# The last weight loads of the first MoE are held back from place 18 of their order instead of place 15

## The chip, the cores and the metric

The kernel runs as one program on one core of a Trainium2 chip. The metric is the device time of the program in microseconds (us). The core has five engines that run side by side and meet through semaphores: PE (TensorE: matrix products into PSUM), DVE (VectorE: elementwise work), ACT (ScalarE: activations), POOL (GpSimd: elementwise work on SBUF) and SP, which here only issues DMA transfers. Each engine and each DMA queue works its instructions off in the order in which they stand in the program; whoever waits holds up all that stands behind it on the same engine.

## What is computed

Three stages follow each other, all in float32 with weights that arrive as 64-bit numbers:

```python
# 1. delta-rule attention, state S per head, t = 0..767
y[t] = q[t] @ S
S    = S + beta[t] * outer(k_n[t], v[t] - k_n[t] @ S)      # k_n: k by its norm
# 2. first MoE: x is the attention's output, 3072 tokens x 384
h = x @ w_in                                              # 384 -> 2048
g = where(h >= 1, h, where(h <= -1, 0, (h + 1)**2 / 4))
x = g @ w_out                                             # 2048 -> 384
# 3. second MoE
xn = x / sqrt(mean(x*x) + 1e-6) * rms_g
out = (silu(xn @ w_gate) * (xn @ w_val)) @ w_out          # 384 -> 1536 -> 384
```

## The kernel before

**Attention.** The 768 steps are cut into 12 chunks of 64, and each chunk into two units, one for each pair of batches, so there are 24 units; unit u belongs to chunk u // 2. Within a unit the recurrence becomes matrix products on PE plus the inverse of a triangular matrix. `a_gram` makes the products of the keys with each other (tile `gk`), scales them (`al`) and stores them to DRAM (`scr_a`). `inverse` works on groups of units (units 0 and 1, units 2 and 3, then four at a time): it loads the stored products as `nt`, runs 31 pairs of steps on POOL (L530, L536), and stores the result (`scr_x`, `scr_a`). `a_mz` reads it back as `tx` and `g` and scales it on POOL into `wt` (L557, L558); `a_mw` multiplies once more on PE (`mg`) and finishes `wt` on DVE (L585). `b_vn` scales the values on POOL (`kvb`, L612). `b_gs` multiplies queries and keys on PE (`gs`, L623) and masks the result on DVE (L629, L633); two such halves to a unit, four to a chunk. `b_tr`, `b_x`, `b_ds` and `b_xT` follow on PE (`tr`, `px`, `ds`, `xps`).

**First MoE.** The weights of one slice f of 128 hidden columns come as two tiles, i = 0 for `w_in` and i = 1 for `w_out`. `w_dec` loads one (`wst`, L265, 384 KB) and decodes it: two activations on ACT, three steps on DVE (L286, L287, L297), one activation, three products on PE (`wlo`, L315 to L317), and one copy (L320 on ACT or L322 on DVE). The number f + 3 i (SK is 3) is the tile's **place** in the order of decoding. From place 10 on, the loads land in four staging buffers that are used in turn, so a load must wait until the DVE step L297 of the tile four loads before it has read its buffer. `m1` then runs for 12 blocks of 256 tokens, one block to a chunk, and for 16 slices each: nine products into `hps`, the gate on ACT and DVE (L773, L781), nine products into `acc`. A group of nine is written "block.slice" below. There are two `hps` buffers, each free again when DVE has done L773. While blocks 0 to 11 run, the weights of the second MoE are decoded too (`w_dec` with n = 2: L286, L287, L290, L291 on DVE) and stored for later.

**Second MoE.** From about 660 us on PE has products alone (`gv`, `acc`), with all weights decoded.

**What sets the order.** All work of attention, first MoE and decoding is written as generators that yield stages. A planner (`Flow`) keeps an estimate of each engine's time and of free buffers, picks the stage that can start next, by its priority, and so fixes the order of instructions on every engine when the program is built. A stage may start when its `needs` are done; a need is therefore an entry in the planner's bookkeeping, no semaphore of its own on the chip. Because each choice depends on those before it, an entry that is changed at one place can move everything that is planned after it.

The loads of `w_dec` for the first MoE have such a need from some place on: `("a_gram", EARLY - 1)`, with EARLY = 8, which is done when the key products of unit 7 have been sent to DRAM. The line is 255. It is the only thing that the diff touches.

Of the kernel before, what the change touches and what calls it, by code (L numbers as in the profile page):

```python
# [160 lines left out]
def kernel_body(  # L161
# [89 lines left out]
    def w_dec(n, f, i):  # L251
        if n == 2:
            needs = [("w_dec", 1, NF1 - 1, 1)]
        else:
            needs = [("a_gram", EARLY - 1)] if f + SK * i > 14 else []
        if n == 1:
            needs = needs + ([("inv0", 1 if f + SK * i < 9 else 19)] if f + SK * i >= 4 else [])
        me = ("w_dec", n, f, i)
# [76 lines left out]
    EARLY = 8  # L335
# [516 lines left out]
    SK = 3  # L852
# [20 lines left out]
    with tc.manual_schedule():  # L873
# [28 lines left out]
        for f in range(NF1):  # L902
            for i in range(2):
                fl.add(f + SK * i + (-14), w_dec, 1, f, i)
        for n, x in enumerate(w2q):
            fl.add(16 + 4 * n, w_dec, 2, *x)
# [168 lines left out]
```

## Time and profile before

| | us |
|---|---|
| median of 3 runs | 1153.7 |
| lowest and highest run | 1152.92, 1155.39 |
| the profiled execution, its own time | 1154.3 |
| its span from first to last instruction | 1152.4 |
| PE busy | 1107.5 |
| DVE busy | 661.8 |
| ACT busy | 569.9 |
| POOL busy | 286.3 |

The profiled execution lies 0.6 us above the median, and 1.9 us of its time lie outside its span. PE is busy nearly all of the time, so what is to be looked for are the few microseconds in which it is not, and those in which it runs at half its clock.

### The profile page before, as it was taken

Reading aid. Unit: us, or ns where it says so; the run is one execution under the profiler, and the core shown is the slowest. Engines: PE = TensorE matmul, PEld = TensorE weight load, DVE = VectorE, ACT = ScalarE, POOL = GpSimd, SP = SyncE. Lnnn points to the kernel's source line nnn. Section 1 sums busy time; section 2 is a strip of 40 time slices with the busy share of each in tenths; the row PEclk is TensorE's granted clock in tenths of the full one; section 3 lists DMA queues with packets and bytes.
Section 4 is the critical chain, followed back from the end, with each engine's and each line's share of the span. In section 5 each row is a group of like instructions: output and inputs, shape, how many; then the busy total and the mean of one; then the engine's idle time right before and its main releaser. Section 6 shows DMA issues by size and latency. Waiting matters only on the chain.

```text
span 1152.4 us, 27191 instructions
## 1 busy us (share of the span) xinstructions
PE 1107.5 (96%) x11224; PEld 996.4 (86%) x11224; DVE 661.8 (57%) x1337; ACT 569.9 (49%) x1360; POOL 286.3 (25%) x479
## 2 busy tenths in 40 slices
PE   8979999999999999999999999999999999999998
PEld 7857888899998999899999999788888888888887
DVE  6797876786877876785775453443433333333333
ACT  4677877765765767567665464222212122122212
POOL 3282865858348114811000000000000000000000
PEclk9989999999999999999999999999999999999999
DMA  7945587784786556385440564001001010010000
GB/s 219 285 143 138 148 262 197 231 208 153 185 224 185 128 199 181 114 206 172 151 148 2 183 207 167 10 23 37 19 1 46 10 37 19 1 46 10 28 1 28
DMA packets 165099, 136.97 MB, mean 119 GB/s; under 512 B 115056, under 2 KB 126064, under 8 KB 164976
## 3 DMA queue, kind: packets, MB, share of 16 engines
q1 hardware_dynamic: 141536, 132.31, 38.2%
q10 hardware_dynamic: 23440, 2.93, 1.7%
q8 instruction: 88, 1.44, 0.5%
q14 instruction: 35, 0.29, 0.1%
HBM read 100.88 MB, written 34.34 MB: 117 GB/s over the span
## 4 chain that ended last, share of the span: by engine, by line
PE 74%; DVE 11%; ACT 4%; POOL 3%; DMA 3%; issue 2%; SPq 1%; DVEq 0%; POOLq 0%; ACTq 0%
PE acc L736 9%; PE gv L736 8%; PE gv L737 8%; PE gv L738 8%; PE acc L737 8%; PE acc L738 8%; PE hps L736 4%; PE hps L737 4%; PE hps L738 4%; PE gs L623 2%; POOL xi L536 2%; PE px L691 2%; POOL tmp L530 2%; PE tr L678 1%; DVE da L287 1%
## 5 line engine op out<-in xcount | busy, mean ns | idle before, releaser
L752 ACT ACTIVATE xh<-fix 128x512 fp32r<-128x512 f32 x72 | 45.5, 632 | 333.7 <-PE acc L738 328.4
L753 DVE TENSOR_TENSOR xl<-fix,xh 128x512 fp32r<-128x512 f32 x72 | 49.9, 694 | 270.6 <-ACT xh L752 270.6
L736 PE MATMUL hps<-xh,w 128*128 128x256 f32 x576 | 167.5, 291 | 9.9 <-DVE w__1065 L773 2.2
L737 PE MATMUL acc<-g,w 128*128 128x256 f32 x576 | 164.7, 286 | 10.6 <-DVE g L781 10.4
L736 PE MATMUL acc<-g,w 128*128 128x256 f32 x576 | 167.8, 291 | 2.7 <-ACT g L779 2.7
L736 PE MATMUL gv<-fix,w 128*128 128x512 f32 x432 | 168.2, 389 | 0.7 <-DVE fix L978 0.7
L737 PE MATMUL gv<-fix,w 128*128 128x512 f32 x432 | 168.1, 389 | 0.0
L738 PE MATMUL gv<-fix,w 128*128 128x512 f32 x432 | 168.1, 389 | 0.0
L737 PE MATMUL hps<-xl,w 128*128 128x256 f32 x576 | 164.2, 285 | 0.0
L738 PE MATMUL hps<-xh,w 128*128 128x256 f32 x576 | 163.9, 285 | 0.0
L738 PE MATMUL acc<-g,w 128*128 128x256 f32 x576 | 163.5, 284 | 0.0
L769 ACT ACTIVATE s<-hps 128x256 f32<-128x256 f32 x192 | 73.6, 384 | 108.3 <-PE hps L738 104.2
L736 PEld LDWEIGHTS hps<-xh,w 128*128 128x128 f32 x576 | 111.2, 193 | 13.7 <-DVE w__1065 L773 2.6
L737 PEld LDWEIGHTS acc<-g,w 128*128 128x128 f32 x576 | 110.7, 192 | 13.0 <-DVE g L781 12.9
L530 POOL TENSOR_TENSOR tmp<-nt,xi 128x87 f32<-128x87 f32 (+21 forms) x186 | 104.4, 561 | 54.5 <-DMA nt<-scr_a 40.4
L736 PEld LDWEIGHTS acc<-g,w 128*128 128x128 f32 x576 | 110.4, 192 | 6.1 <-ACT g L779 2.9
L536 POOL TENSOR_TENSOR xi<-xi,tmp 128x87 f32<-128x87 f32 (+21 forms) x186 | 110.4, 594 | 14.6
L737 PEld LDWEIGHTS hps<-xl,w 128*128 128x128 f32 x576 | 111.4, 193 | 0.3 <-DVE xl L732 0.3
L738 PEld LDWEIGHTS hps<-xh,w 128*128 128x128 f32 x576 | 111.3, 193 | 0.0
L738 PEld LDWEIGHTS acc<-g,w 128*128 128x128 f32 x576 | 110.7, 192 | 0.0
L770 ACT ACTIVATE s<-s,vhalf 128x256 f32<-128x256 f32 x192 | 97.9, 510 | 6.2
L736 PEld LDWEIGHTS gv<-fix,w 128*128 128x128 f32 x432 | 81.1, 188 | 17.8 <-DVE fix L978 1.1
(747 smaller groups left out, 2156.5 us busy)
## 6 DMA issues: line engine op xcount, KB each, us to landing
wst<-in_w SPq DMA_DIRECT2D x68, 384.0 KB, 4.6
w2d<-wst SPq DMA_DIRECT2D x36, 384.0 KB, 4.1
w<-w2d SPq DMA_DIRECT2D x36, 384.0 KB, 6.0
wsv<-in_w SPq DMA_DIRECT2D x36, 383.5 KB, 5.5
kvb<-in_kv SPq DMA_DIRECT2D x22, 384.0 KB, 5.5
kt<-in_kqT SPq DMA_DIRECT2D x24, 256.0 KB, 4.2
scr_a<-al SPq DMA_DIRECT2D x24, 256.0 KB, 3.9
qs<-in_kqT SPq DMA_DIRECT2D x48, 128.0 KB, 4.3
```

What stands on the lines that cost most here:

```text
L287: nc.vector.tensor_scalar(out=a, in0=yf, scalar1=0xFF800000, scalar2=None, op0=ALU.bitwise_and)
L530: nc.gpsimd.tensor_tensor(out=tv, in0=nt[:, m:32, j:m].to_broadcast([w, n, m]), in1=x[:, j:m, 0:m].to_broadcast([w, n, m]), op=ALU.mult,)
L536: nc.gpsimd.tensor_tensor(out=x[:, m:32, 0:m], in0=x[:, m:32, 0:m], in1=tv, op=ALU.add)
L623: nc.tensor.matmul(out=ps[half(b), h, 0:n], lhsT=kt[u][half(1 - b), 4 * k + h, :], rhs=qs[p][half(1 - b), b, 4 * k + h, 0:n], start=True, ...
L691: nc.tensor.matmul(out=ps[half(b), h, 0:D], lhsT=t[:, 0:C], rhs=v, start=True, stop=True)
L736: nc.tensor.matmul(out=out, lhsT=wh, rhs=xh, start=first, stop=False, skip_group_check=shared)
L737: nc.tensor.matmul(out=out, lhsT=wh, rhs=xl, start=False, stop=False, skip_group_check=shared)
L738: nc.tensor.matmul(out=out, lhsT=wl, rhs=xh, start=False, stop=last, skip_group_check=shared)
L752: nc.scalar.activation(out=hi, in_=src, func=ACTF.Copy)
L753: nc.vector.tensor_tensor(out=lo, in0=src, in1=hi.bitcast(F32), op=ALU.subtract)
L769: nc.scalar.activation(out=s, in_=ps, func=IDENTITY_SAT240, scale=240.0)
L770: nc.scalar.activation(out=s, in_=s, func=ACTF.Square, bias=vhalf, scale=1.0 / 480.0)
```

## The change

One number changes. The places are f + 3 i; with the old bound the tiles at places 15, 16, 17 and 18 had to wait in the plan for unit 7's key products, with the new bound only the tile at place 18 has to. The tiles at places 15 to 17 are four: (12,1) and (15,0) at place 15, (13,1) at 16, (14,1) at 17; (15,1) is at 18.

```diff
--- before.py
+++ after.py
@@ -252,7 +252,7 @@
         if n == 2:
             needs = [("w_dec", 1, NF1 - 1, 1)]
         else:
-            needs = [("a_gram", EARLY - 1)] if f + SK * i > 14 else []
+            needs = [("a_gram", EARLY - 1)] if f + SK * i > 17 else []
         if n == 1:
             needs = needs + ([("inv0", 1 if f + SK * i < 9 else 19)] if f + SK * i >= 4 else [])
         me = ("w_dec", n, f, i)
```

Both programs have the same instructions, except for a few DMA issues that are merged or split in the listing; they differ in where these stand. Three places follow.

On SP, from the loads at places 13 and 14 on (the first row ends with them), to the loads of `tx`, `g` and `nt` that feed POOL. Before:

```order
L265 DMA wst<-in_w 128x384 x3
L544 DMA scr_a_557<-xi 16x32x32 x2
L449 DMA scr_a_1227<-al 128x512
L424 DMA ka<-in_kqT 128x2x512
L550 DMA tx<-scr_x_1481 128x1x256
L552 DMA g_1606<-scr_a_557 128x8x32
L550 DMA tx<-scr_x_1481 128x1x256
L552 DMA g_1634<-scr_a_557 128x8x32
L521 DMA nt<-scr_a_1227 32x32x32 x4
L265 DMA wst<-in_w 128x384 x4
```

And after:

```order
L265 DMA wst<-in_w 128x384 x4
L544 DMA scr_a_557<-xi 16x32x32 x2
L449 DMA scr_a_1227<-al 128x512
L265 DMA wst<-in_w 128x384 x3
L550 DMA tx<-scr_x_1491 128x1x256
L552 DMA g_1637<-scr_a_557 128x8x32
L550 DMA tx<-scr_x_1491 128x1x256
L552 DMA g_1656<-scr_a_557 128x8x32
L521 DMA nt<-scr_a_1227 32x32x32 x4
L265 DMA wst<-in_w 128x384
```

The four loads that stood behind `nt` stand ahead of `tx`: one ahead of the stores of the first inverse, three right ahead of `tx`. The load of the keys of units 10 and 11 (`ka`), which stood ahead of `tx`, stands further back.

On PE in chunk 3, at the second unit's `gs` (unit 7): the groups of the first MoE that stand ahead of it and behind it, one row of each (the row with which it begins; "..." stands for the others). Before:

```order
L736 MATMUL hps_3679<-xh_3256,w_593 128x256
...
L623 MATMUL gs_3716<-qs_363,kt_3250 64x112 x8
L623 MATMUL gs_3728<-qs_363,kt_3250 64x112 x8
L436 MATMUL gk_3741<-ka_3432 64x64 x16
L436 MATMUL gk_3765<-ka_3432 64x64 x16
L678 MATMUL tr_3794<-kvb_3207,wt_3663 64x48 x16
L678 MATMUL tr_3817<-kvb_3252,wt_3696 64x48 x16
L736 MATMUL acc0_3641<-g_3677,w_639 128x256
```

And after:

```order
L736 MATMUL hps_3684<-xh_3307,w_593 128x256
...
L736 MATMUL acc0_3646<-g_3674,w_639 128x256
...
L736 MATMUL hps_3720<-xh_3307,w_665 128x256
...
L736 MATMUL acc0_3646<-g_3697,w_714 128x256
...
L623 MATMUL gs_3761<-qs_363,kt_3303 64x112 x8
L623 MATMUL gs_3773<-qs_363,kt_3303 64x112 x8
L436 MATMUL gk_3786<-ka_3487 64x64 x16
L436 MATMUL gk_3810<-ka_3487 64x64 x16
L678 MATMUL tr_3839<-kvb_3260,wt_3699 64x48 x16
L837 MATMUL rps_3891<-sr_3737,ones_r_95 128x256
```

Three groups of nine products (27 rows), which stood behind `tr`, stand ahead of `gs`; the norm's product `rps` now stands right behind `tr`.

On DVE in block 6, around the decoding of two tiles of the second MoE. Before:

```order
L286 SCALAR_TENSOR_TENSOR wst<-dy,da_99 128x384
L287 TENSOR_SCALAR da_99<-wst 128x384
L290 TENSOR_SCALAR wsv<-wsv 128x384
L291 SCALAR_TENSOR_TENSOR wst<-wsv,da_99 128x384
L781 TENSOR_TENSOR g<-w__7674,g 128x256
L585 TENSOR_TENSOR wt<-mg,c_3535 32x8x32 x4
L286 SCALAR_TENSOR_TENSOR wst<-dy,da_100 128x384
L287 TENSOR_SCALAR da_100<-wst 128x384
L290 TENSOR_SCALAR wsv<-wsv 128x384
L291 SCALAR_TENSOR_TENSOR wst<-wsv,da_100 128x384
L773 TENSOR_TENSOR w__7804<-s,hps 128x256
```

And after:

```order
L773 TENSOR_TENSOR w__7693<-s,hps 128x256
L286 SCALAR_TENSOR_TENSOR wst<-dy,da_100 128x384
L287 TENSOR_SCALAR da_100<-wst 128x384
L290 TENSOR_SCALAR wsv<-wsv 128x384
L291 SCALAR_TENSOR_TENSOR wst<-wsv,da_100 128x384
L781 TENSOR_TENSOR g<-w__7693,g 128x256
L773 TENSOR_TENSOR w__7762<-s,hps 128x256
L781 TENSOR_TENSOR g<-w__7762,g 128x256
L773 TENSOR_TENSOR w__7796<-s,hps 128x256
```

Two decodings and the four steps of `wt` stood between two L773; in the new order one decoding stands between L773 and its L781, and the other stands elsewhere.

## Rows read from the trace of the kernel before

**Rows 1.** The page: span, busy time and instructions, and one row of its DMA issues.

```profile
span 1152.4 us, 27191 instructions
...
PE 1107.5 (96%) x11224; PEld 996.4 (86%) x11224; DVE 661.8 (57%) x1337; ACT 569.9 (49%) x1360; POOL 286.3 (25%) x479
...
wst<-in_w SPq DMA_DIRECT2D x68, 384.0 KB, 4.6
```

**Rows 2.** Waits of PE, 90 to 660 us: us in total, times, longest.

```profile
PE acc L737 <- DVE g L781: 4.0, 6, 1.2
PE gs L623 <- DVE wt L585: 2.5, 1, 2.5
...
PE hps L736 <- DVE w__7804 L773: 2.0, 1, 2.0
PE wlo L315 <- DVE xl L732: 1.3, 1, 1.3
...
PE wlo L315 <- DVE w L322: 1.0, 1, 1.0
```

**Rows 3.** Timeline of SP: start, us, what it issues.

```profile
107.14 0.40 SPq L424 DMA_DIRECT2D ka<-in_kqT  x1
107.63 0.58 SPq L550 DMA_DIRECT2D tx<-scr_x  x1
...
110.84 4.88 SPq L521 DMA_DIRECT2D nt<-scr_a  x4
```

**Rows 4.** Timeline of DVE at three places: start, us, operation.

```profile
108.08 0.56 DVE L297 SCALAR_TENSOR_TENSOR w<-wst,da 128x384 fp32r<-128x384 uint32 x1
...
229.91 1.72 DVE L585 TENSOR_TENSOR wt<-mg,c 32x256 f32<-32x256 f32 x4
231.66 0.35 DVE L629 TENSOR_TENSOR kvb<-kvb,gs 128x192 f32<-128x192 f32 x1
...
463.99 0.74 DVE L286 SCALAR_TENSOR_TENSOR wst<-dy,da 128x384 uint32<-128x384 uint32 x1
...
466.23 0.88 DVE L291 SCALAR_TENSOR_TENSOR wst<-wsv,da 128x384 fp32r<-128x384 uint32 x1
```

**Rows 5.** Timeline of POOL; in brackets the idle time before, and what ended it.

```profile
112.35 0.62 POOL L557 TENSOR_TENSOR wt<-tx,c 128x256 f32<-128x256 f32 x1 [8.00 <-DMA tx<-scr_x]
...
160.80 1.62 POOL L612 TENSOR_TENSOR kvb<-kvb,n__1199 128x384 f32<-128x384 f32 x2
...
228.16 0.73 POOL L558 TENSOR_TENSOR wt<-tx,c 128x256 f32<-128x256 f32 x1
```

**Rows 6.** Timeline of PE; x is the number of matmuls merged into the row.

```profile
152.02 3.29 PE L623 MATMUL gs<-qs,kt 64*64 64x112 f32 x64
...
168.43 0.38 PE L736 MATMUL hps<-xh,w 128*128 128x256 f32 x1 [0.61 <-DVE w__2565 L773]
...
227.09 0.28 PE L736 MATMUL hps<-xh,w 128*128 128x256 f32 x1
...
228.05 0.28 PE L738 MATMUL hps<-xh,w 128*128 128x256 f32 x1
230.81 2.50 PE L623 MATMUL gs<-qs,kt 64*64 64x112 f32 x32 [2.48 <-DVE wt L585]
...
237.74 0.38 PE L736 MATMUL acc<-g,w 128*128 128x256 f32 x1
...
314.99 2.08 PE L436 MATMUL gk<-ka 64*64 64x64 f32 x64
...
329.22 2.07 PE L678 MATMUL tr<-kvb,wt 64*64 64x48 f32 x64
...
467.62 0.39 PE L736 MATMUL hps<-xh,w 128*128 128x256 f32 x1 [2.04 <-DVE w__7804 L773]
```

**Rows 7.** Two stretches: length, busy time by engine, granted clock, DMA share, GB/s.

```profile
232.00:233.00 1.00, 1.00 (x15) 1.00 (x14) 0.95 (x4) 0.01 (x1) 0.93 (x2) 0.50 0.38 60
...
468.00:470.00 2.00, 2.00 (x26) 1.70 (x24) 1.94 (x5) 0.91 (x3) 1.76 (x4) 1.00 0.98 301
```

## Prediction

> **What bounds the kernel now.** I read the page first: PE is busy for 1107.5 of the 1152.4 us of the span [rows 1], so the time is PE's work plus its gaps plus what a halved clock costs. The work stays the same here, since both programs hold the same products; only gaps and clock can change. The list of PE's waits came next [rows 2]. Between 90 us, where the new order begins to differ, and 660 us, where PE has products alone, the five largest groups are 4.0, 2.5, 2.0, 1.3 and 1.0 us. All of them end with a DVE step. That is the whole stock from which the change can win, some 11 us, and what it can lose is new entries of the same kind.
>
> Behind the DVE steps stands a slower chain. POOL cannot begin the inverse of a group before `tx` and `nt` have landed: for group 2 it sat idle for 8.00 us until `tx` came [rows 5], and `nt` is issued behind that [rows 3]. Its results are needed by the masks of chunk 2 (`kvb` at 160.80) and by the `wt` of chunk 3 (L558, ending at 228.89) [rows 5]. The longest attention wait of PE is at that second place: the last product ahead starts at 228.05, the next, `gs`, at 230.81 after 2.48 us of idleness, when DVE's L585, started at 229.91, has freed a bank of PSUM [rows 4, 6]. So I price the change there, and follow POOL's chain to it.
>
> **POOL's chain comes 1.4 us later.** In the kernel before, SP issued `tx` at 107.63, right behind `ka` [rows 3]. In the new order three staging loads stand there instead. Each waits for the L297 of the tile four loads before, and the last of the three for the one that runs from 108.08 to 108.64 [rows 4]. With one issue of 0.40 us, as the `ka` row has it, `tx` is issued at 109.0, which is 1.4 us later; `nt` follows at the same distance. The decoding of that older tile is not moved, so it cannot be much earlier. I take 1.4 us for all of POOL's later dates. The lower bound is 0.4 us, if the load needs only to be queued, the upper is in the second rival.
>
> **The early products of the last weights.** The waits of `wlo`, 1.3 and 1.0 us [rows 2], came where four of them stood in a row, with DVE late. The order now has one before `tx`'s products, one right behind, and the rest between groups of the first MoE; their DVE steps move into a stretch around 110 to 120 us in which DVE had waited. I expect 2.3 us less here and some 1 us of new waits for banks. But this isn't kept: the masks of chunk 2 wait for `kvb`, which comes 1.4 us later, and the third group of block 1, at 168.43, waits for DVE behind those masks [rows 5, 6]. By then the same set of products is done in both orders. Two short DVE steps, of some 0.4 us each, no longer stand between the masks, so PE starts it between 0.8 us earlier and 1.4 us later; I take 0.2 us later. The next wait, the longest of the `g` group with 1.2 us [rows 2], has a further group of nine products ahead of it in the new order and should lose 1.0 us of its length. PE then reaches chunk 3 about 0.8 us ahead, between 1.8 us ahead and 0.4 us behind.
>
> **Chunk 3, the main term.** Three groups of nine products now stand ahead of unit 7's `gs`. The products of a group start 0.12 us apart at full clock (227.09 to 228.05 in eight steps) [rows 6], so a group takes 1.08 us and three take 3.24 us. The `gs` itself becomes possible when POOL's L558 is done, 228.89 + 1.4 = 230.3, and L585 begins; it began at 229.91 before and `gs` followed 0.9 us later, so now at 231.2 [rows 4 to 6]. PE comes to it at 228.3 - 0.8 + 3.24 = 230.8 and still waits for 0.4 us. So `gs` starts 0.4 us later than before with 3.24 us more work done: **2.85 us won**. This holds whatever happened earlier, as long as PE comes before 231.2; if PE comes 0.4 us behind the old order (232.0), it is 2.0 us.
>
> **The clock.** After the 2.48 us of idleness the granted clock was 0.50, the lower of its two levels, for the stretch from 232 to 233 [rows 7]. From `gs` to the first `acc`, PE took 237.74 - 230.81 = 6.93 us for 32 `gs`, 64 `gk` and 64 `tr` matmuls. At full clock half of 3.29, and 2.08 and 2.07 us, make 5.8 us by those rows, and 5.7 us without their overlap at the ends [rows 6]. So the low clock cost 1.2 us. The other wait of that size, 2.04 us before 467.62, left the clock at 1.00, the upper level, from 468 to 470 [rows 6, 7], so a wait of 0.4 us should not drop it: **1.2 us won**, bounds 0 and 1.2.
>
> **Behind chunk 3** the three groups are missing as cover. The masks of the four halves start 0.85 us after `gs` (230.81 to 231.66) [rows 4, 6], take some 4.6 us on DVE, and only then come two L773 and the step that makes `sr`, about 1.1 us, for the norm's `rps`, which now stands directly behind `tr`. DVE is there at 231.2 + 0.85 + 4.6 + 1.1 = 237.8, PE at 231.2 + 5.7 = 236.9: **1.0 us lost**, bounds 0 and 1.5.
>
> **Block 6.** The wait of 2.04 us before 467.62 came because DVE had a decoding of 3.1 us (463.99 to 467.11) and the four steps of `wt`, behind another decoding, ahead of L773 [rows 4, 6]. The new order has this pair apart. I take half of it, **1.0 us won** (bounds 0 and 2.0), since where the other decoding stands now it can hold something up as well. Against that I set one new wait of the usual size somewhere in 240 to 660 us, **0.7 us lost**: in the new order the four masks of a chunk stand closer together from chunk 7 on. This term is the least known; the other waits of 0.3 to 1.0 us after 240 us are drawn anew, which I put at 3 us to either side.
>
> **Sum:** -2.85 - 1.2 + 1.0 - 1.0 + 0.7 = -3.35 us. The profiled execution took 1154.3 us, so it would be 1150.95 us; it lies 0.6 us above the median of 1153.7 us, and against the median that is 1150.4 us. A measurement of this kernel can tell about 0.2%, or 2.3 us, from no change; the forecast is just beyond that.
>
> **Rivals.** *First, the gain in chunk 3 is drowned* by the redrawn small waits: the gains of 2.85 and 1.2 us come, the other terms go against it by 3 us, and the time is within 2.3 us of before, 1153.4 us. For it speaks that these are many places and that nothing in the change aims at them; against it that they have no sign of their own.
>
> *Second, the loads ahead of `tx` hold up more than SP's issuing.* Three loads of 384 KB stand directly ahead of it, and such a load takes 4.6 us to land [rows 1]. If `tx` moves only when the last of them has landed, POOL's lateness grows from 1.4 to at most 6.0 us; halfway, at 3.7 us, every date of POOL is 2.3 us later than I have it. Then the wait in chunk 2 grows beyond 2.5 us, and the clock falls there for 1.2 us; PE comes to chunk 3 at 228.3 - 0.8 + 2.3 + 1.2 + 3.24 = 234.2 and `gs` starts 3.4 us later with 3.24 us more done. That gives 0.2 - 1.2 + 1.0 - 1.0 + 0.7 = -0.3 us, 1153.4 us: no change. Against it: in the kernel before, `tx` took 4.7 us from issue (107.63) to POOL's first step (112.35) [rows 3, 5], and not more than a load. The Trainium skill (DMA: Bandwidth & Descriptors, Queues, rings and completion order) says that each DMA engine takes the descriptors of one ring in their order, and that SP has one ring on each engine. By that rule the loads do delay `tx`, and the change would be worth nothing, as in this rival; the rows of before cannot show it, since no load stood directly ahead of `tx`.
>
> *Third, slower: DVE's closer masks.* From chunk 7 on, the order of DVE has six places where three or four mask steps (each 1.15 us: 231.66 and three more in 4.6 us) stand without a gate step between them, two of them with a decoding beside; before, none of these chunks had more than two. That is about six mask steps and two decodings, each of up to 3.1 us, more ahead of an L773: 13 us of DVE work in all. PE has two `hps` buffers and the ready `acc` groups as cover. If half of this shows on PE, it takes 6.4 us in place of my 0.7 us and the sum becomes -3.35 - 0.7 + 6.4 = +2.35 us, the point from which it decides; at 60% it is +3.75 us, 1157.4 us. Against it: the four masks of chunk 3 ran right in a row before, and PE had no wait of over 0.2 us behind them until 237.74, because other attention products covered it.
>
> *Fourth, the change does nothing*, because the planner would issue these loads at the same places anyway. The order excludes it.
>
> **How the numbers follow.** Forecast with its terms: 0.50. First rival: 0.17. Second: 0.15. Third: 0.13. The remaining 0.05 is a gain of over 6 us, if nothing is given back behind chunk 3 and block 6 loses all of its wait. The forecast's own range is 3 us to either side, and a tenth of it falls within 0.2%. Faster by over 0.2%: 0.45 + 0.05 and a little of the second, 0.51. Within 0.2%: 0.05 + 0.15 + 0.12, 0.31. Slower: 0.13 and a part of the first, 0.18. The range reaches from 1146.8, the forecast with its bounds, to 1156.0, which leaves out most of the third rival.
>
> **What would show it.** POOL's first `wt` step at about 113.8 instead of 112.35, and `kvb` at 162.2. No wait of `wlo` of over 1 us. PE's `gs` of unit 7 at about 231 with a wait of under 1 us and a clock of 1.00 behind it, with the `acc` group that followed at 237.74 already done. No wait of 2 us near 467. I am wrong if `tx` lands after 115, if PE waits for over 2 us in chunk 2, or if DVE's masks in chunks 7 to 11 end waits of PE of over 1 us each.

## The result and the profile after

| | before | after |
|---|---|---|
| median of six runs each (us) | 1155.4 | 1162.0 |
| lowest to highest (us) | 1152.9 to 1157.2 | 1160.9 to 1165.2 |
| ratio, 95% interval | | 1.0060, 1.0042 to 1.0079 |
| the profiled execution, its own time (us) | 1154.3 | 1160.9 |
| its span, mean granted clock | 1152.4, 0.993 | 1159.0, 0.987 |

The change made the kernel 0.6% slower, some 7 us. The forecast was 1150.4 us, and the time lies above its range.

The page of after says that PE's work is what it was: 1108.2 us busy where [rows 1] has 1107.5. The 7 us are gaps of PE, and slow clock behind them: outside its busy time PE has 50.8 us of the span, 5.9 more than before, and the mean granted clock is 0.987 instead of 0.993.

```profile
span 1159.0 us, 27225 instructions
...
PE 1108.2 (96%) x11224; PEld 1000.3 (86%) x11224; DVE 665.7 (57%) x1338; ACT 569.2 (49%) x1359; POOL 282.6 (24%) x479
```

Not quite all work stays on its engine: one copy of a decode went from ACT (L320) to DVE (L322), hence the counts of 1338 and 1359.

PE's waits of after from 90 to 660 us (waited for: us in total, times, longest) stand against [rows 2]:

```profile
PE acc L737 <- DVE g L781: 8.7, 10, 2.3
PE wlo L315 <- DVE qs L633: 3.3, 2, 2.8
PE gs L623 <- DVE wt L585: 1.9, 1, 1.9
PE mg L579 <- issue: 1.7, 1, 1.7
PE hps L736 <- DVE w__2613 L773: 1.5, 1, 1.5
PE ds L705 <- issue: 1.4, 1, 1.4
```

The group that grew most is `acc` waiting for the low half of `g`: 8.7 us in ten waits instead of 4.0 in six. Eight of them, 6.7 us, lie after 260 us, where before had 1.1 us in two. All of PE's waits from 90 to 660 us together rose from 20.8 to 25.6 us, nearly all of it (9.2 to 13.4 us) after 260 us. From 260 to 660 us after also has 3.4 us at the lower clock, where before has none. The timeline of DVE of after shows what stands in front of the longest:

```profile
352.67 2.46 DVE L847 SCALAR_TENSOR_TENSOR x<-x,rg,ri 128x256 f32<-128x256 f32 x3
355.05 0.41 DVE L773 TENSOR_TENSOR w__5863<-s,hps 128x256 f32<-128x256 f32 x1
355.38 0.71 DVE L286 SCALAR_TENSOR_TENSOR wst<-dy,da 128x384 uint32<-128x384 uint32 x1
356.12 0.69 DVE L287 TENSOR_SCALAR da<-wst 128x384 uint32<-128x384 uint32 x1
356.73 0.84 DVE L290 TENSOR_SCALAR wsv<-wsv 128x384 uint32<-128x384 uint32 x1
357.61 0.89 DVE L291 SCALAR_TENSOR_TENSOR wst<-wsv,da 128x384 fp32r<-128x384 uint32 x1
358.41 0.94 DVE L781 TENSOR_TENSOR g<-w__5863,g 128x256 fp32r<-128x256 f32 x1
```

Here are two of the rows of PE that end such waits, at this place and 114 us later:

```profile
359.41 0.39 PE L737 MATMUL acc<-g,w 128*128 128x256 f32 x1 [2.30 <-DVE g L781]
...
473.69 0.39 PE L737 MATMUL acc<-g,w 128*128 128x256 f32 x1 [2.04 <-DVE g L781]
```

A decode of a second-MoE tile (L286 to L291, 3.0 us from 355.38 to 358.41) has come between a product's L773 and its L781, behind steps of the norm that had already filled DVE. At 469.5, 484.1 and 497.7 us another decode stands ahead of an L781, between it and its L773 too, but with other steps between that L773 and the decode. That was the first theory; the experiments correct it.

### The profile page after: what moved, and what is told of

It is laid out like the page before. It is cut to its first block, busy times and chain, and to the rows that moved or that the text cites. A ratio compares the mean times of both kernels' runs of the same rounds, so it can differ in the third digit from the quotient of the medians.

```text
span 1159.0 us, 27225 instructions
## 1 busy us (share of the span) xinstructions
PE 1108.2 (96%) x11224; PEld 1000.3 (86%) x11224; DVE 665.7 (57%) x1338; ACT 569.2 (49%) x1359; POOL 282.6 (24%) x479
## 4 chain that ended last, share of the span: by engine, by line
PE 77%; DVE 12%; ACT 4%; DMA 3%; issue 3%; SPq 0%; POOL 0%; DVEq 0%; POOLq 0%; ACTq 0%
PE acc L736 9%; PE acc L737 9%; PE acc L738 9%; PE gv L736 8%; PE gv L737 8%; PE gv L738 8%; PE hps L736 5%; PE hps L738 4%; PE hps L737 4%; PE gs L623 2%; PE px L691 2%; PE tr L678 2%; DVE g L781 1%; PE gk L436 1%; DVE qs L633 1%
## 5 line engine op out<-in xcount | busy, mean ns | idle before, releaser
L737 PEld LDWEIGHTS acc<-g,w 128*128 128x128 f32 x576 | 111.9, 194 | 18.8 <-DVE g L781 18.6
L736 PEld LDWEIGHTS acc<-g,w 128*128 128x128 f32 x576 | 111.6, 194 | 5.6 <-ACT g L779 3.0
L738 PEld LDWEIGHTS acc<-g,w 128*128 128x128 f32 x576 | 111.9, 194 | 0.0
```

Of the source, the lines that this page charges most:

```text
L736: nc.tensor.matmul(out=out, lhsT=wh, rhs=xh, start=first, stop=False, skip_group_check=shared)
L737: nc.tensor.matmul(out=out, lhsT=wh, rhs=xl, start=False, stop=False, skip_group_check=shared)
L738: nc.tensor.matmul(out=out, lhsT=wl, rhs=xh, start=False, stop=last, skip_group_check=shared)
```

## The experiments

Most kernels keep the program and fix the order of its instructions. The planner's picks are written out as a list, and the kernel takes from it the first step that can start; PE's order is that of the kernel the list was taken from, wherever nothing else is said.

```diff
-plan = Flow.step
+ORDER = (...)                  # the planner's steps of one kernel, one after the other
+def listed(fl):                # the first of ORDER that can start; once it is empty, the planner
+    ...
+plan, Flow.step, Flow.todo = Flow.step, listed, None
```

**Which stretch loses.** The two orders were grafted onto each other near 300 us:

```diff
-ORDER = AFTER
+ORDER = [s for s in AFTER if s.t < 296] + [s for s in BEFORE if s not in head]   # e1; e2 the other way round
```

> The changed kernel's order of instructions up to about the end of chunk 4 (near 300 us), and from there on the order of the kernel before; no instruction is added or left out. Theory A (the loss is made by the order of the products, copies and decodes after 300 us, which the planner drew anew): the time comes back to the kernel before's, 1155.4 us, within 2 us (ratio 0.998 to 1.002). Theory B (the four earlier loads in the head leave an engine or a queue late, and the tail only pays for it): it stays at the changed kernel's 1162 us (ratio 1.004 to 1.008).

Measured: ratio 1.0009 (0.9996 to 1.0022), +1.0 us.

> The opposite graft: the order of the kernel before up to near 300 us, so with the four loads where they were, and then the changed kernel's order. Theory A (the order after 300 us loses): 1160 to 1163 us (ratio 1.004 to 1.007), although the loads are not early at all. Theory B (the early loads lose, by way of the head): 1155.4 us within 2 us (ratio 0.998 to 1.002).

Measured: 1.0062 (1.0039 to 1.0085), +7.2 us, with the loads where they always were. Its `acc` waits from 260 to 640 us are close to after's (6.3 us against 6.7, the longest 2.3 us in both), and the 1.2 us of `rps` are after's too. The 2.6 us of `hps`, at 306 us, stand at the seam of the two orders and are in neither kernel:

```profile
PE acc L737 <- DVE g L781: 6.3, 6, 2.3
PE hps L736 <- DVE w__4987 L773: 2.6, 1, 2.6
PE rps L838 <- DVE sr L834: 1.2, 1, 1.2
```

So the order after 300 us loses by itself, without any early load, and the head, with the early loads, is level. Theory A holds, though up to 2.6 of the 7.2 us can be the seam's.

**The loads alone.**

```diff
-ORDER = BEFORE
+ORDER = BEFORE with the loads of (12,1), (15,0), (13,1), (14,1) at their places in AFTER   # SP only
```

> The kernel before with nothing moved but the four loads of places 15 to 17 on SP, which stand where the changed kernel has them (one ahead of the load of `ka`, three ahead of the first `tx`); PE, DVE, ACT and POOL keep the order of the kernel before. Theory A (the early loads by themselves cost next to nothing, the loss is in the redrawn order after 300 us): 1153 to 1156.5 us (ratio 0.998 to 1.001); a gain within that is the waits of wlo at 131 and 136 us (2.3 us of wait before), which the earlier data would shorten. Theory B (the loads ahead of `tx` hold up the key chain on POOL and all that follows): 1157 to 1159 us (ratio 1.0015 to 1.003).

Measured: 1.0013 (1.0000 to 1.0026), +1.5 us, between the ranges of the two theories, so it decides for neither. In its trace SP issued the three loads within 1.46 us and `tx` right behind, and POOL's first `wt` step began at 118.56 us, 6.2 us later than [rows 5]. Still the time rose by 0.1% only: even with a POOL chain far later than I had forecast, the loss is a fifth of the change's.

```profile
109.71 1.46 SPq L265 DMA_DIRECT2D wst<-in_w  x3
111.23 0.59 SPq L550 DMA_DIRECT2D tx<-scr_x  x1
```

**A new draw, with and without loads.** Bounds 15 and 16 free two and three of the four loads. Two controls move no load, but set one engine of the planner's book later once.

```diff
-            needs = [("a_gram", EARLY - 1)] if f + SK * i > 14 else []
+            needs = [("a_gram", EARLY - 1)] if f + SK * i > 15 else []   # e8; e12: > 16
```

```diff
-ORDER = BEFORE
+ORDER = [s for s in BEFORE if s.t < 160]       # e11: 112
+fl.free["DVE"] += 1.5                          # once, when ORDER is empty; e11: "POOL", 1.8
```

> The bound is 15 instead of 14 or 17: two of the four loads (both at place 15) are set free, the rest waits for unit 7's key products as before; the planner draws the whole order anew. Theory A, in its form that the loads don't matter and each new draw gets its own small waits: the time is not in proportion; it lies anywhere from 1153 to 1163 us, and its waits after 300 us stand at other places than in either kernel. Theory B (the time follows how many loads are early): between the two kernels, 1157 to 1160 us, with the loss before 300 us.

> The bound is 16: three of the four loads are set free. Theory A2: a third draw, not in proportion to the number of loads, anywhere from 1154 to 1163 us, with its waits after 300 us at places of its own. Theory B (the time follows how many loads are early): between bound 15 (1158.4 us) and the changed kernel (1162 us), so 1159 to 1162 us.

> A control: the kernel before with its loads where they were and its order kept up to 160 us of the plan; there the planner's book for DVE is set 1.5 us later, once, and it draws the rest anew. No early load anywhere. Theory A2 (a new draw of the order after some point loses by itself, because its small waits fall elsewhere): slower than before, 1157 to 1163 us (ratio 1.001 to 1.007). Rival G (only what the four early loads set going, POOL's chain later against the blocks, makes a losing order): 1154 to 1157 us (ratio 0.999 to 1.001).

> A second control: the kernel before with its loads where they were and its order kept up to 112 us of the plan; there the planner's book for POOL is set 1.8 us later, once, which is by how much the four loads set POOL's chain back in the plan of the changed kernel. Theory A2: slower, 1157 to 1163 us (ratio 1.001 to 1.007). Rival G: slower as well, and like the changed kernel, 1160 to 1163 us (ratio 1.004 to 1.007); so this control tells only whether the lateness of POOL's chain alone is enough.

Measured: bound 15, 1.0018 (1.0004 to 1.0032); bound 16, 1.0000 (0.9982 to 1.0018); the DVE control 1.0055 (1.0030 to 1.0080); the POOL control 0.9986 (0.9971 to 1.0002). With none, two, three and four loads early the ratio is 1, 1.0018, 1.0000 and 1.0060: no proportion. Bound 15 lies inside the ranges of both theories, and theory B falls with bound 16; theory A's range for a new draw was so wide that it could hardly miss. A control without any early load loses as much as the change, the other nothing. Both theories had expected the second to be slower, and both missed; so POOL's lateness in the plan is not enough by itself to make an order lose. The DVE control has its largest wait here, two decodes in a row, 6.6 us of DVE, ahead of the `xl` that PE's `gs` needs:

```profile
356.52 0.78 DVE L286 SCALAR_TENSOR_TENSOR wst<-dy,da 128x384 uint32<-128x384 uint32 x1
...
362.17 0.97 DVE L291 SCALAR_TENSOR_TENSOR wst<-wsv,da 128x384 fp32r<-128x384 uint32 x1
...
363.84 1.02 DVE L732 TENSOR_TENSOR xl<-xps,xh 128x384 fp32r<-128x384 f32 x2
```

The row of its waits from 240 to 660 us that this makes:

```profile
PE gs L623 <- DVE xl L732: 3.8, 1, 3.8
```

**Is it the place between L773 and L781?**

```diff
-ORDER = AFTER                                   # e4: BEFORE
+ORDER = AFTER with each decode that stood right between an L773 and an L781 put right behind that L781
```

> The changed kernel's order with 14 decodes of the second MoE moved on DVE: each stood between a product's L773 and the next L781 and now stands right behind that L781; nothing else moves. Theory C (PE's waits of acc for g, 6.7 us from 300 to 660 us in the changed kernel, are the decode standing in front of L781): 4 to 6 us are won, 1156 to 1158 us (ratio 1.001 to 1.002 against the kernel before). Rival (the waits only move from L781 to the next L773, so to hps, or the loss lies in the attention matmuls that start late without a releaser): 1160 to 1163 us (ratio 1.004 to 1.007).

> The kernel before with the same move at its 11 places of that kind. Theory C: its waits of acc behind such decodes in the blocks up to 500 us, 1.1 us at 354 and 2.2 us at 465, go: 1152 to 1154 us (ratio 0.997 to 0.999). Rival (the wait is only handed on to the next L773): 1155.4 us within 1 us (ratio 0.999 to 1.001).

Measured: 1.0070 (1.0049 to 1.0092) and 1.0038 (1.0018 to 1.0058), both on the rival's side or beyond it: theory C fell. e3 by itself tests it at one of the four costly places only, since the decodes at 469.5, 484.1 and 497.7 us did not stand right behind an L773 and kept their places, and their waits stayed (1.90, 0.54 and 0.79 us). In e3 the `acc` wait at 359 us is gone and a wait of `hps` stands in its place, for the L773 behind the decode; e4 got a new one of 3.07 us. First the row of e3's PE, then, from e4's timelines, PE's new wait and the decode ahead of it on DVE:

```profile
360.01 0.39 PE L736 MATMUL hps<-xh,w 128*128 128x256 f32 x1 [2.45 <-DVE w__5909 L773]
```

```profile
388.25 0.39 PE L736 MATMUL hps<-xh,w 128*128 128x256 f32 x1 [3.07 <-DVE w__6432 L773]
```

```profile
383.38 0.96 DVE L286 SCALAR_TENSOR_TENSOR wst<-dy,da 128x384 uint32<-128x384 uint32 x1
384.38 1.55 DVE L287 TENSOR_SCALAR da<-wst 128x384 uint32<-128x384 uint32 x1
385.85 1.42 DVE L290 TENSOR_SCALAR wsv<-wsv 128x384 uint32<-128x384 uint32 x1
387.30 0.56 DVE L291 SCALAR_TENSOR_TENSOR wst<-wsv,da 128x384 fp32r<-128x384 uint32 x1
387.78 0.41 DVE L773 TENSOR_TENSOR w__6432<-s,hps 128x256 f32<-128x256 f32 x1
```

At either place the decode (3.3 us in e3, 4.4 us in e4) stands in front of something that PE needs, and the step behind it is late.

**Take the decode out of the stretch, or shorten it.** In e6 four decodes of after leave their places (355.4, 469.5, 484.1, 497.7 us), later ones move up into the place behind, and four new places follow near 600 us. In e7 three of before do so (344.9, 368.2, 464.0 us). In e9 nothing moves, but two of the four DVE steps of those four decodes are left out.

```diff
-ORDER = AFTER                                   # e7: BEFORE
+ORDER = AFTER with the decode places of (5,0), (8,1), (8,2), (9,0) dropped and four added at the end
```

```diff
-        nc.vector.tensor_scalar(out=a, in0=yf, scalar1=0xFF800000, scalar2=None, op0=ALU.bitwise_and)
+        if n == 1 or (f, i) not in CUT: nc.vector.tensor_scalar(out=a, in0=yf, scalar1=0xFF800000, scalar2=None, op0=ALU.bitwise_and)
...
-            nc.vector.tensor_scalar(out=v, in0=v, scalar1=0x1FFFFFF, scalar2=None, op0=ALU.bitwise_and)
+            if (f, i) not in CUT: nc.vector.tensor_scalar(out=v, in0=v, scalar1=0x1FFFFFF, scalar2=None, op0=ALU.bitwise_and)
```

> The changed kernel with the four decodes of the second MoE that stand on DVE at 355.4, 469.5, 484.1 and 497.7 us of its trace taken out of those places: every later decode takes the place of the one behind it, and four new places follow near 600 to 630 us. PE's and POOL's orders stay as they are. Theory D (DVE has more work in these stretches than PE's products leave time for, with the POOL running beside it and the decodes at 3.1 to 3.6 us each; the decode is what PE waits on, whatever stands first): PE's waits of 2.5, 2.2, 0.8 and 0.95 us there go, and the time is 1155.5 to 1157.5 us (ratio 1.000 to 1.002). Rival E (the waits are tied to the order of PE's own products against the attention's, and reappear behind the next DVE step): 1160 to 1163 us (ratio 1.004 to 1.007).

> The changed kernel in its own order, with two of the four DVE instructions (L287 and L290) left out of the four decodes of the second MoE at 355.4, 469.5, 484.1 and 497.7 us, so that part of three weight tiles' low halves and their sums is not formed; loads, stores, ACT's part and every other instruction stay. Theory D (what PE waits for there is DVE's time alone): the waits of 2.5, 2.2, 0.8 and 0.95 us fall by the left-out 1.5, 1.5, 1.0 and 1.4 us, down to zero at most, which is 4.7 us: 1156.5 to 1158.5 us (ratio 1.001 to 1.003). Rival F (what was won by taking these decodes away came from their loads, stores and activations): 1161 to 1163 us (ratio 1.005 to 1.007).

> The same for the kernel before: the three decodes that stand on DVE at 344.9, 368.2 and 464.0 us of its trace are taken out, with three new places near 610 to 630 us; PE's and POOL's orders stay. Theory D: its waits of 0.8, 1.1, 0.8 and 2.2 us in these stretches go, and the time is 1150.5 to 1153 us (ratio 0.996 to 0.998), less than either kernel. Rival E: 1155 to 1156.5 us (ratio 0.999 to 1.001).

Measured: e6 1.0011 (0.9992 to 1.0029); e9 1.0021 (0.9998 to 1.0044); e7 0.9949 (0.9936 to 0.9962), median 1150.7 us. e6 and e9 came out as theory D had it: moving the four decodes wins back 0.5% of the 0.6%, and leaving out 5.5 us of their DVE steps wins back 0.4%. e7 won more than the theory's 0.2 to 0.4%: the kernel before had a loss of this kind in it too. **e7 beats both kernels** here, by 0.5% and 1.1%. The first two rows here are e7's `acc` and longest `hps` waits from 260 to 640 us; before had 2.0 us in one place [rows 2].

```profile
PE acc L737 <- DVE g L781: 0.9, 1, 0.9
PE hps L736 <- DVE w__6406 L773: 0.7, 1, 0.7
```

**Chunk 3.** The wait of `gs` that I forecast at 0.4 us was 1.9 us. In after, DVE reached L585 only behind a decode, 3.3 us from 230.29 on:

```profile
230.29 0.97 DVE L286 SCALAR_TENSOR_TENSOR wst<-dy,da 128x384 uint32<-128x384 uint32 x1
...
233.10 0.56 DVE L291 SCALAR_TENSOR_TENSOR wst<-wsv,da 128x384 fp32r<-128x384 uint32 x1
233.58 1.72 DVE L585 TENSOR_TENSOR wt<-mg,c 32x256 f32<-32x256 f32 x4
```

f1, f2 and f4 also drop this decode's place, from after, from e6 and from e7:

```diff
-ORDER = AFTER                                   # f2: e6's, f4: e7's
+ORDER = AFTER with the decode place of (2,0) dropped and one added at the end
```

> The changed kernel with one decode of the second MoE taken out of its place on DVE, the one from 230.29 to 233.6 us that stands in front of chunk 3's L585; later decodes each take the place of the one behind, and one new place follows near 620 us. Theory D (the decode, not POOL's chain, set the date of `gs` in chunk 3): L585 begins when POOL's L558 has ended, near 230.9 at the latest, `gs` becomes possible by 231.8 and PE, which comes at 232.4, no longer waits; 1.9 us are won there and up to 1.7 us of low clock behind: 1158.5 to 1160.5 us (ratio 1.003 to 1.005). Rival H (POOL's later chain holds `gs` anyway, or PE's lead is taken back at the next wait): 1161 to 1163 us (ratio 1.005 to 1.007).

> The changed kernel with this decode and the four of 355 to 500 us taken out of their places, and five new places near 595 to 630 us. Theory D: what both moves won adds up: 1153 to 1155.5 us (ratio 0.998 to 1.000). Rival H: as with the four alone, 1156.5 to 1158 us (ratio 1.001 to 1.003).

> The kernel before with the three decodes taken out as in the fast version of it, and with the one from 227.16 to 229.9 us, in front of chunk 3's L585, taken out as well; four new places near 600 to 630 us. Theory D: `gs` of unit 7 becomes possible behind POOL's L558 (228.9 us), so its wait of 2.5 us shrinks to about 1.5 us and the clock behind it may stay up: 1.0 to 2.2 us less than the 1150.7 us of the three alone, 1148.5 to 1150 us (ratio 0.994 to 0.9955). Rival H: no change against that version, 1150 to 1151.5 us (ratio 0.995 to 0.9965).

Measured: f1 1.0051 (1.0039 to 1.0063), f2 1.0017 (0.9997 to 1.0037), f4 0.9980 (0.9967 to 0.9994). The wait itself went: f1 has no wait of `gs` in chunk 3, and f4 one of 0.2 us. The time hardly followed, as rival H had it for f1 and f2: f1 is some 1 us under after, within both intervals, and f2 is no better than e6. f4 missed both ranges: it has e7's edit in it, and yet its interval lies above e7's. So of e7's gain only 0.2% came back in f4; whether the rest is lost by the added move or was never e7's, these runs don't settle, nor where the 1.9 us of f1 went.

**POOL beside DVE.**

```diff
-            nc.gpsimd.tensor_tensor(
+            if g not in (5, 6): nc.gpsimd.tensor_tensor(
...
-            nc.gpsimd.tensor_tensor(out=x[:, m:32, 0:m], in0=x[:, m:32, 0:m], in1=tv, op=ALU.add)
+            if g not in (5, 6): nc.gpsimd.tensor_tensor(out=x[:, m:32, 0:m], in0=x[:, m:32, 0:m], in1=tv, op=ALU.add)
```

> The changed kernel in its own order, without the 31 pairs of POOL steps (L530, L536) of the last two of the seven inverse groups, so units 16 to 23 get the identity in place of their inverse; their loads and stores stay. POOL is then idle from about 338 to 375 and 450 to 490 us. Theory D2 (the decodes on DVE take 3.1 to 3.6 us there because POOL works beside them, and 1.8 us otherwise): each decode in these stretches falls to 1.8 to 2.0 us, the waits of 2.5, 2.2 and 0.8 us shrink to under 1 us each, and the time is 1156 to 1158.5 us (ratio 1.001 to 1.003). Rival I (the decodes are as slow without POOL): their durations and the waits stay, 1161 to 1163 us (ratio 1.005 to 1.007).

> The kernel before in its own order, without the 31 pairs of POOL steps (L530, L536) of the last two of the seven inverse groups, so units 16 to 23 get the identity in place of their inverse; their loads and stores stay. Theory D2 (the 7 us between the two orders are DVE steps slowed by POOL, met at worse places in one order than in the other): both orders come out alike, 1148 to 1152 us, within 2.5 us of the 1150.5 us of the changed kernel with the same cut. Rival J (the order of before is better in itself, by its products and copies): it keeps its lead of 5 to 8 us, 1142.5 to 1145.5 us.

Measured: f3 0.9959 (0.9943 to 0.9975), 1150.5 us; f5, the same in before, 0.9937 (0.9915 to 0.9960), 1148.6 us. Both kernels leave out the POOL steps of two inverses. I had expected 1156 to 1158.5 us of f3; but without POOL's work the other DVE steps that read SBUF alone are faster too (the three L847 here 1.26 us, in after 2.46). The decode that took 3.0 us in after, in f3:

```profile
343.68 1.26 DVE L847 SCALAR_TENSOR_TENSOR x<-x,rg,ri 128x256 f32<-128x256 f32 x3
344.86 0.41 DVE L773 TENSOR_TENSOR w__5841<-s,hps 128x256 f32<-128x256 f32 x1
345.19 0.55 DVE L286 SCALAR_TENSOR_TENSOR wst<-dy,da 128x384 uint32<-128x384 uint32 x1
345.77 0.36 DVE L287 TENSOR_SCALAR da<-wst 128x384 uint32<-128x384 uint32 x1
346.05 0.35 DVE L290 TENSOR_SCALAR wsv<-wsv 128x384 uint32<-128x384 uint32 x1
346.44 0.56 DVE L291 SCALAR_TENSOR_TENSOR wst<-wsv,da 128x384 fp32r<-128x384 uint32 x1
346.91 0.42 DVE L781 TENSOR_TENSOR g<-w__5841,g 128x256 fp32r<-128x256 f32 x1
```

It takes 1.72 us. The lead of before shrinks from 7 us to 2.5 us (0.9959 less 0.9937, of 1155 us; the intervals reach from about none to 6 us). So most of the difference, perhaps not all, was DVE slowed by POOL at worse places in one order than in the other; rival J's lead of 5 us lies just within the interval and is not excluded.

## Why the prediction was wrong, step by step

- **What bounds the kernel** was right in the main: PE's work is the same, and of the 4.2 us by which its waits after 260 us grew, 3.7 end with a DVE step. Before 260 us it is otherwise: the new wait of `mg` (1.7 us) ends with no DVE step, and the clock fell to 0.50 behind it. The stock was misread as well. Waits of `wlo` on L633, 2.1 us in two, belong among the five largest of before, and all waits of before from 90 to 660 us make 20.8 us, not 11.
- **POOL's chain 1.4 us later** was right at its start and not behind it. `tx` was issued at 109.34 us (forecast 109.0) and POOL's first `wt` step began at 114.21 (113.8). But the `kvb` of chunk 2 came at 161.35, only 0.55 us later than before (162.2 forecast), and the L558 of chunk 3 ended at 229.33, 0.44 us later.
- **The second rival** had a mechanism that is there and a price that is not. From the issue of `tx` to POOL's first step it took 4.87 us in after, where [rows 3, 5] have 4.7, but 7.3 us in e5, where the loads were issued in one burst ahead of it. The Trainium skill (DMA: Bandwidth & Descriptors, Queues, rings and completion order) says that each DMA engine consumes the descriptors of a ring in order. The 7.3 us of e5 agree with that; the 4.87 us of after, with the same loads issued over 3.24 us, hardly show it. Yet e5 as a whole cost 1.5 us, so this isn't where 7 us went.
- **The early products** were half right. The waits at 131 and 136 us are gone, but the wait of `wlo` that ends at 110 us, which the forecast had left out, grew from 1.5 to 2.8 us. Behind it the clock fell to 0.50, where before it had stayed at 1.00. First before's row, then after's and its clock:

```profile
109.81 0.88 PE L315 MATMUL wlo<-dy,ident 128*128 128x384 f32 x2 [1.52 <-DVE qs L633]
...
110.03 1.62 PE L315 MATMUL wlo<-dy,ident 128*128 128x384 f32 x2 [2.80 <-DVE qs L633]
...
110.00:111.00 1.00, 0.97 (x3) 0.70 (x3) 0.93 (x3) 0.49 (x1) 0.00 (x0) 0.50 0.95 286
```

- **Chunk 3, 2.85 us and 1.2 us of clock**, is the first step that failed. I let POOL's L558 set the date of L585. But L585 in [rows 4] shows no idle time ended by POOL. In before, too, it stood in DVE's queue right behind a decode, from 227.16 to 229.9 us, and in after it does so until 233.58. The wait was 1.9 us, not 0.4 (PE came at 232.6 instead of 230.8), and the clock fell to 0.50 again. Together with the loss of 1.0 us behind chunk 3 (by its own dates 0.9) the head was to win 3.05 us; e1 measured +1.0 us (-0.5 to +2.5). The decode in before, and `gs` and the clock in after:

```profile
227.16 0.56 DVE L286 SCALAR_TENSOR_TENSOR wst<-dy,da 128x384 uint32<-128x384 uint32 x1 [0.34 <-ACT da L276]
...
229.14 0.85 DVE L291 SCALAR_TENSOR_TENSOR wst<-wsv,da 128x384 fp32r<-128x384 uint32 x1
...
234.47 2.55 PE L623 MATMUL gs<-qs,kt 64*64 64x112 f32 x32 [1.86 <-DVE wt L585]
...
236.00:237.00 1.00, 1.00 (x16) 1.00 (x14) 0.95 (x4) 0.00 (x0) 0.73 (x1) 0.50 0.92 145
```

- **Block 6**: its wait of 2.04 us [rows 6] did go, and another of 2.04 us, at 473.69, came, behind the decode from 469.50 us on. The term was worth nothing, and behind the new wait the clock fell as well.
- **One new wait of 0.7 us, with 3 us to either side for all the others**, is the step that decided. With block 6 I had -0.3 us after 300 us; e2 measured +7.2 us (4.5 to 9.8, the seam's wait included), and the traces show 4.2 us more of waits after 260 us and 3.4 us at the lower clock. I priced many re-sorted places as noise around zero with a width that I had no row for. The order in fact showed the decodes standing between L773 and L781, and [rows 4] showed that such a decode takes 3.1 us; I used that for the place where one went away, not for those where one came. Counting alone would not have done: such a place right between L773 and L781 is there 14 times in after and 11 times in before.
- **The third rival** had the right sign and engine, and its point of 1157.4 us was the nearest to 1162. Its mechanism was wrong in the main: the masks from chunk 7 on end no wait of 1 us in after, and the trace has three places with three or four masks and no gate step between them, not six. The decodes, which it counted beside the masks, were what PE's longest waits stood behind.

What stays open: e6 and e7, each without its worst decodes, still lie 0.6% apart, as far as after and before do. Moving the worst decodes away won in either order, so e6 and e9 show what these decodes cost after, and not that their places make up the difference from before; f3 and f5 bear on that, with the width said. The clock of every execution points at where the rest lies. 38 executions of before had a mean granted clock of 0.993 and a mean span of 1152.5 us, 11 had 0.988 and 1156.4 us: 0.8 us for each 0.001. The six of after are at 0.985 on average, all 122 of before beside the experiments at 0.992. By an estimate from these numbers some 5 of the 7 us go with time at the lower clock, and likewise most of what lies between e6 (0.986) and e7 (0.994). In the traces the low clock comes behind waits of PE, so this counts partly the same us as the gaps. It shows what goes together, and not yet a cause: which of the waits bring the clock down was tested by no run.

## What to carry to other kernels

When one number makes a planner sort a program anew, the new order can be a draw, as here: controls that touched nothing of the subject landed at 0.9986 and 1.0055. Run such a control before a change of half a per cent is credited to what it was for. For the forecast, go through the order engine by engine for the long movable steps (here the decodes), and price each where it has come to stand, at the duration that it has beside the engine that slows it.

## What the runs showed of the hardware

**DVE slows beside POOL, but not in every step.** Means from the DVE rows of after between 240 and 650 us, by whether POOL was busy for under 10% or over 90% of the instruction:

| line | what it reads | POOL idle (us, rows) | POOL busy (us, rows) |
|---|---|---|---|
| L286 | two SBUF tiles | 0.56 (17) | 0.90 (6) |
| L291 | two SBUF tiles | 0.56 (16) | 0.89 (7) |
| L781 | two SBUF tiles | 0.42 (77) | 0.78 (15) |
| L847 | two SBUF tiles | 0.48 (13) | 0.80 (7) |
| L773 | SBUF and PSUM | 0.42 (73) | 0.41 (27) |
| L585 | SBUF and PSUM | 0.41 (18) | 0.41 (6) |
| L712 | SBUF and PSUM | 0.56 (24) | 0.55 (3) |

The one-input steps L287 and L290 slow as well (0.36 us with POOL idle; up to 1.55 us in the rows of e4 above, beside POOL steps of 0.8 to 1.3 us). f3 shows the same by taking POOL's work away. The Trainium skill (SBUF — State Buffer, SBUF: two separate sides) says that DVE and GpSimd share one pair of ports, which one instruction holds to its end, and that DVE wants it for two SBUF inputs or in its two-port modes. Of the lines with two inputs those slow here that take both from SBUF, which agrees; that L287 and L290 run in a two-port mode, no run shows.

**The clock fell behind some waits and not others.** Stretches of after (length, busy by engine, granted clock, DMA share, GB/s), behind the wait of 2.30 us at 359.41 and that of 2.04 us at 473.69:

```profile
360.00:361.00 1.00, 1.00 (x11) 1.00 (x10) 0.97 (x3) 0.93 (x3) 0.92 (x2) 1.00 0.72 236
...
475.00:476.00 1.00, 1.00 (x6) 1.00 (x6) 0.97 (x2) 0.00 (x0) 0.92 (x2) 0.50 0.90 307
```

The longer wait left the clock at the upper level, the shorter one dropped it to the lower; before, 2.04 us had left it up [rows 7]. So a wait of 2 us has two prices here, and I had given new waits the cheap one.
